# Pacing the transposing DMAs of a planned attention and feed-forward kernel

## The chip, the core and the metric

One NeuronCore of one Trainium2 chip runs the whole kernel. Time is device time in microseconds (us) of one execution; a kernel's time is the median of several executions. Kernel before: 416.09 us, median of 3 runs (414.84 to 416.85).

## What is computed

Eight batches of grouped attention (16 query heads, 4 key/value heads, 384 positions, head size 64), whose output goes through a feed-forward layer with a squared ReLU (1024 to 2048 to 1024). All in float32 outside; the tolerance lets the kernel work in 16 bits.

```python
def _attn_ref(q, k, v):                      # q (8,16,384,64), k and v (8,4,384,64)
    k = np.repeat(k, 4, axis=1); v = np.repeat(v, 4, axis=1)
    scores = np.matmul(q, k.transpose(0, 1, 3, 2)) / np.sqrt(64)
    scores = scores - np.max(scores, axis=-1, keepdims=True)
    attn = np.exp(scores)
    attn = attn / (np.sum(attn, axis=-1, keepdims=True) + 1e-09)
    return np.matmul(attn, v)

def _moe_ref(x, w_in, w_out):                # x (3072,1024)
    h = np.maximum(x @ w_in, 0.0)
    return h * h @ w_out
```

## The kernel before

**A planner writes the order.** The kernel is not written as a sequence of instructions. A class `Recorder` (L9) collects operations with what they read and write, and keeps a planned clock for each engine. `R.add` (L45) gives an operation a start and an end in that plan from a cost in us that the code states; `R.when` (L36) says when given data will be there by the plan. Main loops ask which piece of TensorE work can start now by the plan and record it. In the end `emit` (L86) writes one instruction stream per engine in the order of recording, with semaphore waits where data or buffers require them. So a cost or a due time in the code decides the order that the hardware then runs with its own durations.

**The engines' parts.** TensorE (PE) does all matmuls. ScalarE (ACT) does the exponentials (L402), part of the evictions from PSUM, ReLUs and squares. VectorE (DVE) does most evictions, the normalisation of attention, sums, and some squares. GpSimd (POOL) issues the loads of q, k and v (L239, L264, L271), makes some copies, ReLUs and squares. The sync engine (SP) issues the transposing DMAs, here called turns, and the stores of the output (L933); it takes its queue in order.

**One batch of attention.** Its k, q and v are loaded into `k_st`, `q_st`, `v_st`. Then `prepare(b)` (L1027) puts chores on a list: `dup_k` (L295) copies k twice side by side, `turn_k_dma` (L308) turns it into `kT` with one transposing DMA, two `turn_q_dma` (L315) turn the halves of q into `qT`, and `aug_v` (L304) copies v. When the list is empty, `turned` is set to this batch, and its scores may be recorded. The scores are 18 pieces per batch (`burst_small`, L385), each followed by one exponential on ScalarE into `expT`. `av_halves` (L446) multiplies by v in 8 pieces, VectorE normalises, and `turn_o_dma` (L477) turns the result into `xT` with four more DMAs on SP.

**One batch of the feed-forward layer.** For batches 2 to 7 (SB is 2) the up projection is one level of Strassen's scheme (`strassen`, L744): 28 units, each evicted by `evict` (L765). Four products of each column group end in a ReLU and a square; `close_squares` (L675) decides by the planned clocks where they run. Its plans are named by two letters, the engine of the ReLU and that of the square: "ss" is ScalarE for both, "sg" ScalarE and GpSimd, "gg" GpSimd for both, and "sv", which exists only where no ReLU is left, puts the square on VectorE. The plan with the earliest end is taken. The down projection (`down_halves`, L841) follows and reads the squares `h2T`; its pieces run through `zipped` (L712), whose matmuls have line L802 in the up part and L852 in the down part. Attention of the batches ahead is put between these pieces: scores of batch b may be recorded when the feed-forward layer is at batch b-2 or later, its products with v at batch b-1 or later.

**Upkeep.** Before each step the main loops call `upkeep` (L1108) with the planned clock of TensorE. It records loads of the next batch: for batches 4 to 7 as six pieces (`load_pieces`: k, four of q, v), each waiting for the TensorE operation recorded last (`pe_last`) and at least `LOAD_GAP` = 2.0 us of planned time after the one before. Then, while the first chore's data is expected within 0.5 us, it records chores, several in one call where it can. So the k turn and both q turns of a batch are recorded back to back, and each starts when its data and buffers allow. Scores of a batch are candidates in the last main loop (L1308) from the time at which `R.when` expects their turned data.

Of the kernel before, what the change touches and what calls it, by code (L numbers as in the profile page):

```python
# [141 lines left out]
def bass_gqa_attention__then__ffn_squared_relu_kernel(  # L142
# [24 lines left out]
    SB = 2  # L167
    TINY, DOWN = 2.0 ** -100, 2.0 ** -12

    def at(b):  # L170
        return 1 if b == 1 else 0

    R = Recorder(nc)
# [6 lines left out]
    k_dup = sb("k_dup", [128, NU, 2, D])  # L180
# [6 lines left out]
    hr = [sb(f"hr{i}", [128, S], f32) for i in range(NHR)]  # L187
# [16 lines left out]
    q_st = [sb("q_st", [128, H, NJ * D]).ap(), lead(0, 3072, (H, NJ * D))]  # L204
    qT = [sb("qT", [128, 2 * NU, 128]).ap(), lead(3072, 6144, (2 * NU, 128))]
# [99 lines left out]
        R.add(eng, lambda e: e.tensor_copy(v_aug[b % 2][:, :, 0:D], v_st[at(b)][:, :, :]),  # L305
              reads=[("v_st", at(b))], writes=[("v_aug", b % 2)], cost=0.4 if eng == "vector" else 0.85)

    def turn_k_dma(b):  # L308
        R.add("sync", lambda e: e.dma_start_transpose(
            out=kT[at(b)], in_=k_dup.ap().rearrange("p n x d -> p (n x d)")),  # L310
            reads=[("k_dup", 0, g, x) for g in range(HKV) for x in range(2)],
            writes=[("kT", at(b), g) for g in range(HKV)],
            dma="turn_k", cost=1.4, shared=(8.5, 3.5))

    def turn_q_dma(b, half, after=()):  # L315
        R.add("sync", lambda e: e.dma_start_transpose(
            out=qT[at(b)][:, 12 * half:12 * half + 12, :],
            in_=q_st[at(b)][:, 8 * half:8 * half + 8, :].rearrange("p h e -> p (h e)")),
            reads=[("q_st", at(b), 2 * half + i, x) for i in range(2) for x in range(2)] + list(after),
            writes=[("qT", at(b), 2 * half + i, t) for i in range(2) for t in range(6)], dma=f"turn_q{half}", cost=2.5, shared=(10.0, 4.0))  # L320

    def turn_k_pe(b, g, banks):
        i = pick(banks)
# [53 lines left out]
    def score_reads(b, u, c0=0, n=HC):  # L377
        g = u // NJ
        return [("kT", at(b), g)] + [("kT", at(b), g // 2 * 2, x, y) for x in range(2) for y in range(2) if b == 1] + [("qT", at(b), g, t) for t in range(c0 // 128, (c0 + n) // 128)]
# [295 lines left out]
    def close_squares(which):  # L675

        for x in [x for x in open_squares if which(x)]:
            open_squares.remove(x)
            i, r, dst, keys, relu = x
            val = hr[r].ap()  # L680
            two = val.rearrange("p (f t) -> p f t", f=2)
            end = R.ops[i]["end"]
            act, dve, pool = [max(R.clock[e], end) for e in ("scalar", "vector", "gpsimd")]
            plans = [(act + 0.45 * (1 + relu), "ss"), (max(act + 0.52 * relu, pool) + 0.77 + 0.2, "sg")]
            if relu:
                plans.append((pool + 2.2 + 0.6, "gg"))
            else:
                plans.append((dve + 0.49 + 0.4 + 0.6 * bool(ff["now"]), "sv"))
            one, other = min(plans)[1]
            if relu and one == "s":  # L690
                R.add("scalar", lambda e, val=val: e.activation(val, val, AF.Relu, scale=DOWN * DOWN),  # L691
                      reads=[("hr", r)], writes=[("hr", r)], cost=0.45)
            elif relu:
                R.add("gpsimd", lambda e, val=val: e.tensor_scalar(val, val, DOWN * DOWN, 0.0, ALU.mult, ALU.max),
                      reads=[("hr", r)], writes=[("hr", r)], cost=1.42)
            if other == "s":
                R.add("scalar", lambda e, dst=dst, two=two: e.activation(dst, two, AF.Square),  # L697
                      reads=[("hr", r)], writes=keys, cost=0.45)
            else:
                eng = dict(g="gpsimd", v="vector")[other]  # L700
                n = R.add(eng, lambda e, dst=dst, two=two: e.tensor_tensor(dst, two, two, ALU.mult),
                          reads=[("hr", r)], writes=keys, cost=0.77 if other == "g" else 0.49)
                if other == "v":
                    hr_read[r] = (n,)

# [272 lines left out]
    def warm_up(n, cost):  # L978
        def body(pe):
# [8 lines left out]
          reads=[("k_f32", 0)], writes=[("k_dup", 0, 0, 0)], cost=0.27)  # L988
# [38 lines left out]
    def prepare(b):  # L1027

        chores.append(([("k_st", at(b))], lambda: dup_k(b)))
        chores.append(([("k_dup", 0, 0, 0)], lambda: turn_k_dma(b)))  # L1030
        for half in range(2):
            chores.append(([("q_st", at(b), 2 * half, 0)], lambda half=half: turn_q_dma(b, half)))
        chores.append(([("v_st", at(b))], lambda: aug_v(b, "gpsimd")))
        top_q.append(([("v_st", at(b))], lambda: (top_of(v_st[at(b)].rearrange("p n d -> p (n d)"), ("v_st", at(b))),
                                                  spread_q.append((b, lambda: v_unit(b))))))
# [24 lines left out]
    def open_bank(banks):  # L1060
        return min(R.when(writes=[("bank", i)]) for i in banks)
# [41 lines left out]
    margin = 0.5  # L1103
    since, AMONG = 9, 2
    AV_IN, SC_LATE, SC_IN = 4, 2, 8
    load_pieces, load_at, pe_last, LOAD_GAP = [], [0.0], [], 2.0

    def upkeep(now):  # L1108
        nonlocal loaded, queued, turned
        pe_last[0:1] = [len(R.ops) - 1 - next(i for i, o in enumerate(reversed(R.ops)) if o["eng"] == "tensor")]  # L1110
        if loaded + 1 < B and turned >= loaded and not turn_q and not load_pieces:
            loaded += 1
            if loaded == 2:
                load_k(2)
                load_w_out(1, 0)
                load_w_out(1, 1)
                load_q(2, 0, 8)
                load_q(2, 8, 16)
                load_v(2)
                return False  # L1120
            after = [("qT", (loaded - 1) % 2, HKV - 1, 1)] if loaded > 2 else []
            n = loaded
            if n <= SB + 1:
                load_k(n, after)
                load_q(n, 0, 8)
                load_q(n, 8, 16)
                load_v(n)
            else:
                load_pieces.append(([("k_st", 0)], lambda g: load_k(n, after, g)))
                load_pieces.extend(([("q_st", 0, h // 4, x) for x in range(2)], lambda g, h=h: load_q(n, h, h + 4, after=g))  # L1130
                                   for h in range(0, H, 4))
                load_pieces.append(([("v_st", 0)], lambda g: load_v(n, g)))
        if load_pieces and now >= load_at[0] and R.when(writes=load_pieces[0][0], eng="none") <= now:
            load_pieces.pop(0)[1](tuple(pe_last[0:1]))
            load_at[0] = now + LOAD_GAP
        if not chores and not load_pieces and queued < loaded and (queued - (queued == 1), NU - 1, 5) in scored and pairs >= queued * 8 + 8 * (queued == 1):
            queued += 1
            prepare(queued)
        stretch[0] = split and ff["b"] < SB or bool(ff["now"])
        while chores and R.when(reads=chores[0][0], eng="none") <= now + margin:  # L1140
            chores.pop(0)[1]()
            if not chores:
                turned = queued
        if top_q and (ff["b"] < SB or not ff["now"]) and R.when(reads=top_q[0][0], eng="none") <= now + margin:
            top_q.pop(0)[1]()
        while turned > 1 and held_back:
            held_back.pop(0)()
        close_squares(lambda x: not ff["now"] or R.ops[x[0]]["end"] <= now + 0.2)
        if w_q and w_q[0][0]() and R.when(reads=w_q[0][1], eng="none") <= now and R.clock["vector"] <= now + 0.1:
            w_q.pop(0)[2]()  # L1150
        b = next_sum()
        if b and R.when(reads=[("xT", b % NXT, c) for c in range(NKC)], eng="none") <= now + 0.3:
            summed.add(b)
            sums(b)
        return True
# [152 lines left out]
    while ff["now"] or ff["tiles"] or ff["down"]:  # L1308
# [26 lines left out]
        if sc_q:  # L1335
            b, u = sc_q[0]
            pieces = later[u]
            tiles = {(b, x, t) for x, c0, n in pieces for t in range(c0 // 128, (c0 + n) // 128)}
            bases = [i for i in (0, 2) if not held & {i, i + 1}]
            if turned >= b and b <= ff["b"] + 2 and pairs // 2 * NJ + NEX > b * NU + max(x for _, x, _ in tiles) and bases:  # L1340
                base = min(bases, key=lambda i: max(open_bank([i + x]) for x in range(2)))
                t = max(R.when(reads=[r for p in pieces for r in score_reads(b, *p)]), max(open_bank([base + i]) for i in range(2)))
                cand.append((t, 3, "sc", since_sc >= ((SC_LATE if b == ff["b"] + 1 else SC_IN) if inside else 1)))
        if not cand:
            b = next_sum()
# [66 lines left out]
```

## Time and profile before

| | us |
|---|---|
| median of 3 runs | 416.09 (414.84 to 416.85) |
| the profiled execution, whole | 415.26 |
| its span, first to last instruction | 413.5 |
| last transposed output of batch 7's attention issued | 351.42 |

The profile is of one execution. In its lists a line such as L392 is a line of the kernel: L392 scores, L402 exponentials, L459 products with v, L802 and L852 the two halves of the feed-forward layer, L781 and L786 evictions, L691 and L694 ReLUs, L697 and L701 squares. PEld is TensorE's weight load. A wait is told as who waited for whom; "issue" stands where the profile shows no releaser. "DVE hr L781" means that VectorE's instruction of line 781, which writes the tile `hr`, ended the wait. q, k and v are turned at these times in batches 4 to 7: the k turn of each is issued at 159.84, 198.91, 229.94 and 272.07 us.

### The profile page before, as it was taken

What the parts mean: (1) busy time and instruction counts of PE and PEld (TensorE: products, weight loads), DVE (VectorE), ACT (ScalarE), POOL (GpSimd) and SP (SyncE); (2) the same over time, 40 slices, a digit from 0 to 9 for tenths busy, and PEclk for the clock granted to TensorE, in tenths of its full rate; (3) what the DMA queues carried; (4) which work ended last, traced back from release to release, by engine and by line L of the source; (5) the groups of instructions that cost most, each with busy time, mean ns of one, the idle gap of its engine ahead of it and who ended that gap; (6) DMA issues with size and microseconds to landing.
All of it is one profiled execution on the core that took longest, in us unless ns stands there. A gap on an engine that the chain in (4) does not pass through costs nothing.

```text
span 413.5 us, 14959 instructions
## 1 busy us (share of the span) xinstructions
PE 402.5 (97%) x6880; PEld 298.5 (72%) x6880; DVE 268.7 (65%) x519; ACT 225.6 (55%) x316; POOL 79.3 (19%) x92
## 2 busy tenths in 40 slices
PE   8999999998999999999899999999999999999997
PEld 5566754554648985498755898779987899779844
DVE  3699988999977865368732676427861487337613
ACT  6949610196005883777789378935797066006600
POOL 7680000351210450304030063000220000000000
PEclk9999999999999999999999999999999999999999
DMA  9999999992991119972984795263211221220012
GB/s 176 185 192 188 205 187 177 242 149 42 177 193 54 22 22 111 182 153 22 131 114 103 157 152 65 70 127 113 36 28 52 105 41 24 70 76 31 4 51 103
DMA packets 97072, 44.76 MB, mean 108 GB/s; under 512 B 77424, under 2 KB 90992, under 8 KB 97008
## 3 DMA queue, kind: packets, MB, share of 16 engines
q0 software_dynamic: 36672, 17.44, 33.5%
q1 hardware_dynamic: 59664, 25.86, 29.5%
q8 instruction: 54, 0.88, 0.9%
q10 hardware_dynamic: 672, 0.49, 0.4%
q14 instruction: 10, 0.08, 0.1%
HBM read 35.65 MB, written 12.58 MB: 117 GB/s over the span
## 4 chain that ended last, share of the span: by engine, by line
PE 73%; DMA 14%; DVE 6%; POOL 3%; ACT 2%; issue 1%; SPq 0%; POOLq 0%; DVEq 0%
PE ps L852 27%; PE ps L802 24%; DMA w_out_sb<-in_moe_w_out_dram 9%; PE ps L909 9%; PE ps L392 5%; PE ps L459 5%; DMA wx<-in_v_dram 2%; PE ps L554 2%; DVE h2T L578 1%; DMA qT<-q_st 1%; DMA v_st<-in_v_dram 1%; DVE hr L567 1%; PE ps L418 1%; DVE wx L657 1%; ACT h2T L697 1%
## 5 line engine op out<-in xcount | busy, mean ns | idle before, releaser
L402 ACT ACTIVATE expT<-ps 128x1024 bf16<-128x1024 f32 (+1 forms) x145 | 142.2, 1024 | 60.4 <-PE ps L392 57.7
L852 PE MATMUL ps<-w_out_sb,h2T 64*128 64x512 bf16 x1088 | 136.8, 376 | 0.3 <-ACT h2T L697 0.3
L852 PEld LDWEIGHTS ps<-w_out_sb,h2T 64*128 64x128 bf16 x1088 | 73.5, 94 | 37.5 <-ACT h2T L697 0.8
L802 PE MATMUL ps<-xT,w_in_sb 64*128 64x192 f16 x1152 | 82.6, 243 | 0.6 <-issue 0.5
L930 DVE TENSOR_SCALAR y_sb<-ps,unit 128x512 f32<-128x512 f32 (+2 forms) x37 | 29.4, 796 | 68.8 <-PE ps L852 62.2
L802 PEld LDWEIGHTS ps<-xT,w_in_sb 64*128 64x128 f16 x1152 | 71.0, 94 | 2.2 <-issue 0.8
L392 PE MATMUL ps<-qT,kT 64*128 64x256 bf16 (+2 forms) x336 | 51.9, 324 | 3.6 <-issue 1.7
L802 PE MATMUL ps<-s_sum,wx 64*128 64x192 f16 x768 | 50.9, 243 | 1.0 <-DVE hr L781 0.9
L909 PE MATMUL ps<-w_out_sb,h2T 128*128 128x512 bf16 (+2 forms) x240 | 49.7, 365 | 0.6 <-DVE hr L567 0.5
L786 DVE TENSOR_TENSOR hr<-ps,hr 128x384 f32<-128x384 f32 x72 | 39.5, 555 | 12.7 <-PE ps L802 9.5
L802 PEld LDWEIGHTS ps<-s_sum,wx 64*128 64x128 f16 x768 | 43.8, 94 | 2.3 <-DVE hr L781 1.9
L554 PE MATMUL ps<-xT,w_in_sb 64*128 64x384 bf16 x448 | 42.2, 323 | 0.8 <-DVE hr L567 0.8
L778 ACT COPY hr<-ps 128x384 f32<-128x384 f32 x21 | 10.0, 478 | 57.4 <-PE ps L802 57.4
L909 PEld LDWEIGHTS ps<-w_out_sb,h2T 128*128 128x128 bf16 x240 | 22.3, 98 | 25.8 <-DVE hr L567 0.8
L697 ACT ACTIVATE h2T<-hr 128x384 bf16<-128x384 f32 x74 | 37.8, 521 | 2.5 <-DVE hr L773 0.6
L781 DVE COPY hr<-ps 128x384 f32<-128x384 f32 x51 | 27.9, 556 | 17.0 <-PE ps L802 15.6
L459 PE MATMUL ps<-v_aug,expT 64*128 64x65 bf16 x1440 | 37.8, 190 | 0.0
L691 ACT ACTIVATE hr<-hr 128x384 f32<-128x384 f32 x63 | 32.2, 511 | 9.4 <-DVE hr L786 9.4
L459 PEld LDWEIGHTS ps<-v_aug,expT 64*128 64x128 bf16 x1440 | 34.7, 94 | 2.3 <-DVE o_sb L474 0.2
L554 PEld LDWEIGHTS ps<-xT,w_in_sb 64*128 64x128 bf16 x448 | 22.1, 94 | 15.8 <-DVE hr L567 1.9
L802 PE MATMUL ps<-s_sum,w_in_sb 64*128 64x192 f16 x384 | 32.5, 243 | 0.0
L802 PE MATMUL ps<-xT,wx 64*128 64x192 f16 x384 | 31.7, 243 | 0.0
(86 smaller groups left out, 421.3 us busy)
## 6 DMA issues: line engine op xcount, KB each, us to landing
out_dram<-y_sb SPq DMA_DIRECT2D x47, 256.0 KB, 2.9
w_in_sb<-in_moe_w_in_dram POOLq DMA_DIRECT2D x8, 512.0 KB, 14.9
w_out_sb<-in_moe_w_out_dram POOLq DMA_DIRECT2D x4, 1024.0 KB, 29.5
q_st<-in_q_dram POOLq DMA_DIRECT2D x19, 192.0 KB, 5.0
q_st<-in_q_dram POOLq DMA_DIRECT2D x4, 384.0 KB, 24.7
v_st<-in_v_dram POOLq DMA_DIRECT2D x7, 192.0 KB, 5.5
k_st<-in_k_dram POOLq DMA_DIRECT2D x6, 192.0 KB, 4.7
wx<-in_q_dram POOLq DMA_DIRECT2D x2, 384.0 KB, 7.3
```

The source lines that it names most:

```text
L392: mm = pe.matmul(ps[:, base + x, m * wide:(m + 1) * wide], kT[at(b)][64 * x:64 * x + 64, u, :], q_cols(b, u // NJ, x, c0, c0 + wide))
L402: R.add("scalar", lambda e: e.activation(dst, src, AF.Exp, scale=0.125), reads=keys, writes=[("expT", (b * NU + u) % NEX, t) for u, _, _ i ...
L459: m = pe.matmul(ps[:, p[x], n * DP:n * DP + D + 1], w, v_aug[b % 2][r, g * NJ + j, 0:D + 1], start=(n + j + y == 0), stop=(n + j + y == 2 ...
L554: m = pe.matmul(bank(4 + xs[x])[:, 0:S], w_in_sb[r, kc, c * 128:(c + 1) * 128], xT[b % NXT][r, kc, :], start=(phase < 2 and kc == 0), stop ...
L691: R.add("scalar", lambda e, val=val: e.activation(val, val, AF.Relu, scale=DOWN * DOWN), reads=[("hr", r)], writes=[("hr", r)], cost=0.45)
L697: R.add("scalar", lambda e, dst=dst, two=two: e.activation(dst, two, AF.Square), reads=[("hr", r)], writes=keys, cost=0.45)
L781: R.add("vector", lambda e: e.tensor_copy(hr[r][:, :], src), reads=[("bank", at)], writes=[("hr", r)], cost=0.48, after=hr_read.pop(r, ()))
L786: R.add("vector", lambda e: e.tensor_tensor(hr[r][:, :], src, hr[r][:, :], ALU.add), reads=[("bank", at), ("hr", r)], writes=[("hr", r)], ...
L802: return lambda pe: pe.matmul(bank(at)[:, f * h:f * h + h], w[r, kc, c:c + 128], m[r, kc, :], start=(prod in (1, 5, 2) and y + f + kc == 0 ...
L852: return lambda pe: pe.matmul(bank(at)[:, 0:512], h2T[r, c, i3 * 128:(i3 + 1) * 128], w_out_sb[r, c, x * 512:(x + 1) * 512], start=(y + c ...
L909: m = pe.matmul(bank(i)[:, 0:n], h2T[:, c, i3 * 128:(i3 + 1) * 128], w_out_sb[:, c, c0:c1], start=(c == 0), stop=(c == NFC - 1))
L930: R.add("vector", lambda e: e.tensor_scalar(ysl, bank(i)[:, 0:n], g, g, ALU.mult, ALU.mult), reads=[("bank", i), ("unit", b % 2)], writes= ...
```

## The change

Four edits, all in the planner's rules; the arithmetic is the same.

- Batches 4 to 7 (`b > SB + 1`): the k turn and the q turns carry a wait for the TensorE operation recorded last, and after each the shared time `dma_at` is set to 3.5 us (`TURN_GAP`) past TensorE's planned clock. A paced chore is not recorded before that time.
- Load pieces and paced turns share that time: `load_at` is replaced by `dma_at`, so loads also keep 3.5 us from a turn, and turns 2.0 us from a load.
- Scores of batches 4 to 7 in the last main loop are candidates 3.0 us later than the plan expects their data.
- A square on VectorE is priced at 0.95 us instead of 0.49, both in the choice and in the recorded cost.

```diff
-    def turn_k_dma(b):
+    def turn_k_dma(b, gate=()):
         R.add("sync", lambda e: e.dma_start_transpose(
...
-            dma="turn_k", cost=1.4, shared=(8.5, 3.5))
+            dma="turn_k", cost=1.4, shared=(8.5, 3.5), after=gate)
...
-    def turn_q_dma(b, half, after=()):
+    def turn_q_dma(b, half, after=(), gate=()):
...
-            writes=[...], dma=f"turn_q{half}", cost=2.5, shared=(10.0, 4.0))
+            writes=[...], dma=f"turn_q{half}", cost=2.5, shared=(10.0, 4.0), after=gate)
...
-                plans.append((dve + 0.49 + 0.4 + 0.6 * bool(ff["now"]), "sv"))
+                plans.append((dve + 0.95 + 0.4 + 0.6 * bool(ff["now"]), "sv"))
...
-                          reads=[("hr", r)], writes=keys, cost=0.77 if other == "g" else 0.49)
+                          reads=[("hr", r)], writes=keys, cost=0.77 if other == "g" else 0.95)
...
-        chores.append(([("k_dup", 0, 0, 0)], lambda: turn_k_dma(b)))
+        paced = b > SB + 1
+
+        def go(turn, *args):
+            turn(b, *args, gate=tuple(pe_last) if paced else ())
+            if paced:
+                dma_at[0] = R.clock["tensor"] + TURN_GAP
+
+        chores.append(([("k_dup", 0, 0, 0)], lambda: go(turn_k_dma), paced))
         for half in range(2):
-            chores.append(([("q_st", at(b), 2 * half, 0)], lambda half=half: turn_q_dma(b, half)))
+            chores.append(([("q_st", at(b), 2 * half, 0)], lambda half=half: go(turn_q_dma, half), paced))
...
-    load_pieces, load_at, pe_last, LOAD_GAP = [], [0.0], [], 2.0
+    load_pieces, dma_at, pe_last, LOAD_GAP, TURN_GAP = [], [0.0], [], 2.0, 3.5
...
-        if load_pieces and now >= load_at[0] and R.when(writes=load_pieces[0][0], eng="none") <= now:
+        if load_pieces and now >= dma_at[0] and R.when(writes=load_pieces[0][0], eng="none") <= now:
             load_pieces.pop(0)[1](tuple(pe_last[0:1]))
-            load_at[0] = now + LOAD_GAP
+            dma_at[0] = now + LOAD_GAP
...
-        while chores and R.when(reads=chores[0][0], eng="none") <= now + margin:
+        while chores and R.when(reads=chores[0][0], eng="none") <= now + margin and not (len(chores[0]) > 2 and chores[0][2] and now < dma_at[0]):
...
-                t = max(R.when(reads=[r for p in pieces for r in score_reads(b, *p)]), max(open_bank([base + i]) for i in range(2)))
+                t = max(R.when(reads=[r for p in pieces for r in score_reads(b, *p)]) + 3.0 * (b > SB + 1), max(open_bank([base + i]) for i in range(2)))
```

More of the change, by code (lines that the diff above doesn't have):

```diff
@@ L319, in turn_q_dma @@
             reads=[("q_st", at(b), 2 * half + i, x) for i in range(2) for x in range(2)] + list(after),
-            writes=[("qT", at(b), 2 * half + i, t) for i in range(2) for t in range(6)], dma=f"turn_q{half}", cost=2.5, shared=(10.0, 4.0))
+            writes=[("qT", at(b), 2 * half + i, t) for i in range(2) for t in range(6)], dma=f"turn_q{half}", cost=2.5, shared=(10.0, 4.0), after=gate)
     def turn_k_pe(b, g, banks):
```

## The prediction

> **What bounds the kernel now.** I read the page's busy times first, then the table by stage, then TensorE's waits from 126 us on, where every batch that the change touches is computed.
>
> ```profile
> span 413.5 us, 14959 instructions
> PE 402.5 (97%) x6880; PEld 298.5 (72%) x6880; DVE 268.7 (65%) x519; ACT 225.6 (55%) x316; POOL 79.3 (19%) x92
> ...
> 126.00:155.00 29.00, 28.91 (x719) 26.71 (x720) 21.75 (x43) 23.55 (x34) 10.35 (x9) 1.00 0.13 34
> 155.00:177.00 22.00, 22.00 (x314) 11.44 (x312) 9.78 (x20) 11.82 (x12) 4.48 (x6) 1.00 0.99 155
> 177.00:203.00 26.00, 25.09 (x744) 24.21 (x740) 20.54 (x42) 20.47 (x34) 5.70 (x6) 1.00 0.53 77
> 203.00:229.00 26.00, 24.28 (x258) 13.78 (x256) 9.24 (x19) 21.56 (x24) 4.54 (x6) 1.00 0.73 126
> 229.00:254.00 25.00, 23.46 (x702) 22.61 (x699) 18.41 (x41) 15.36 (x28) 7.23 (x8) 1.00 1.03 143
> ```
>
> Columns of the stages: length, then busy time of PE, PEld, DVE, ACT, POOL, granted clock, DMA share, GB/s. I chose the cuts so that an up projection (the Strassen products, 126:155, 177:203, 229:254) and a down projection (between them) alternate. TensorE is the bound: it is busy for the whole of 155:177 and within 2 us of the whole elsewhere, at clock 1.00. The change adds and removes no matmul, so it can only fill or open holes on TensorE. The holes:
>
> ```profile
> PE ps L392 <- issue: 1.7, 1, 1.7
> PE ps L392 <- DMA qT<-q_st: 1.0, 1, 1.0
> PE ps L802 <- DVE hr L781: 0.9, 1, 0.9
> PE ps L802 <- issue: 0.5, 1, 0.5
> PE ps L852 <- ACT h2T L697: 0.3, 1, 0.3
> ```
>
> These five (total, times, longest) are all that the view of TensorE's waits has after 126 us: 1.7 + 1.0 + 0.9 + 0.5 + 0.3 = 4.4 us, 1.1% of the span. That is the ceiling of any gain.
>
> **The turns and the scores: the first two holes.** For batch 5:
>
> ```profile
> 198.91 2.11 SPq L309 DMA_TRANSPOSE kT<-k_dup  x1
> 201.12 4.77 SPq L316 DMA_TRANSPOSE qT<-q_st  x2
> 205.94 1.48 SPq L479 DMA_TRANSPOSE xT<-o_sb  x1
> ...
> kT<-k_dup SPq DMA_TRANSPOSE x1, 5.5
> qT<-q_st SPq DMA_TRANSPOSE x1, 6.1
> ...
> 204.59 1.02 PE L852 MATMUL ps<-w_out_sb,h2T 64*128 64x512 bf16 x7
> 207.34 0.39 PE L392 MATMUL ps<-qT,kT 64*128 64x512 bf16 x2 [1.72 <-issue]
> 208.41 0.40 PE L392 MATMUL ps<-qT,kT 64*128 64x512 bf16 x2
> ```
>
> SP issues the k turn at 198.91 and the first q turn at 201.12; from issue to landing they take 5.5 and 6.1 us, so q lands at 207.2 and the first score matmul starts at 207.34. The view calls this hole "issue", but its end is the landing. Batch 6:
>
> ```profile
> 229.94 2.03 SPq L309 DMA_TRANSPOSE kT<-k_dup  x1
> 232.07 3.48 SPq L316 DMA_TRANSPOSE qT<-q_st  x2
> ...
> 232.07 5.50 DMA qT<-q_st
> ...
> 237.61 0.39 PE L392 MATMUL ps<-qT,kT 64*128 64x512 bf16 x2 [1.01 <-DMA qT<-q_st]
> ```
>
> Here the q turn lands at 232.07 + 5.50 = 237.57. Call T the issue of the k turn: q's first half is there at T+8.3 (batch 5) and T+7.6 (batch 6). The planner's costs in the code, with no load in flight, expect it at 0.1 + 0.8 + 1.4 + 2.5 + 1.5 = T+6.3. So the plan is 2.0 and 1.3 us too early, and the holes are 1.72 and 1.01: the same cause twice.
>
> With the change, the q half is recorded 3.5 us after the k turn, behind a wait for TensorE's latest work. The plan then expects it at 3.5 + 0.1 + 0.8 + 2.5 + 1.5 = T+8.4, and the added 3.0 puts the first score at T+11.4. By the row of 6.1 it lands at T+9.6, so 1.8 us are spare. If another SP issue stands ahead of it (1.48, the xT turn above), 0.3 is left; with the second half's share of 4.77 there as well nothing is, and about 1 us of the wait would come back. I take the full gain, **-1.72 and -1.01**, since each turn now stands alone, and keep 0 for the range.
>
> What the waits hold up: behind a gated turn in SP's queue stand stores and the xT turns of the batch before. The turn at 205.94 is batch 4's last, and its reader starts here:
>
> ```profile
> 228.80 0.24 PE L802 MATMUL ps<-xT,w_in_sb 64*128 64x192 f16 x1
> ```
>
> That is 22.9 us after issue, so a delay by the spread of 7 us costs nothing; uncovered, the whole 7 us would stand on TensorE.
>
> **What is late next.** Scores start at T+11.4 instead of T+6.3, 5.1 us later. TensorE has other matmuls to run, so the delay moves work and adds none. Where the exponentials go:
>
> ```profile
> L402 ACT ACTIVATE expT<-ps x10: 1005/1023/1031, 176.8 to 197.0; 128x1024 bf16<-128x1024 f32 x10
> ...
> 126.00:155.00 29.00, 15.75 (x16) 1.00 0.13 34
> 155.00:177.00 22.00, 10.46 (x11) 1.00 0.99 155
> 177.00:203.00 26.00, 9.98 (x10) 1.00 0.53 77
> 203.00:229.00 26.00, 18.41 (x18) 1.00 0.73 126
> 229.00:254.00 25.00, 4.67 (x5) 1.00 1.03 143
> ```
>
> In a down stage a score comes every 1.07 us (207.34 to 208.41), in an up stage every 2.2 us (ten from 176.8 to 197.0). Five of batch 4's scores slip from 155:177 to 177:203, which then has 15. The stage 126:155 already carries 16 exponentials and ACT 23.55 of 29.00 us, with PE 28.91 busy, so I cost this at **0**. The cover is ACT's free 26.0 - 20.47 = 5.5 us against 5 x 1.02 = 5.1.
>
> **Loads.** Batch 6's loads and the turn after them:
>
> ```profile
> 207.90 0.74 POOL L271 DMA_DIRECT2D q_st<-in_q_dram  x1 [9.48 <-PE ps L392]
> ...
> 216.45 0.74 POOL L264 DMA_DIRECT2D v_st<-in_v_dram  x1 [1.40 <-PE ps L392]
> ```
>
> Pieces already came about 2 us apart and the last was issued 13.5 us before the turn at 229.94. Now the six start at T+10.5 and end at T+20.5. The next T may then come from T+26 by the loads, or from T+11.4 + 18 x 1.07 = T+30.7 by the scores; the measured step is 229.94 - 198.91 = 31.0. Batch 6 may slip by several us, inside the 22.9 of slack: **0**.
>
> **Squares.** The third hole:
>
> ```profile
> L701 DVE TENSOR_TENSOR h2T<-hr x13: 548/550/1195, 139.5 to 390.7; 128x384 bf16<-128x384 f32 x13
> L701 POOL TENSOR_TENSOR h2T<-hr x9: 826/827/1232, 137.8 to 304.1; 128x384 bf16<-128x384 f32 x9
> ...
> 189.47 1.46 POOL L300 COPY k_dup<-k_st 128x1536 bf16<-128x1536 bf16 x1
> 190.88 1.15 POOL L305 COPY v_aug<-v_st 128x768 bf16<-128x768 bf16 x1
> 190.36 2.08 DVE L701 TENSOR_TENSOR h2T<-hr 128x384 bf16<-128x384 f32 x2
> 193.16 1.08 PE L802 MATMUL ps<-s_sum,wx 64*128 64x192 f16 x22 [0.91 <-DVE hr L781]
> ...
> L697 ACT ACTIVATE h2T<-hr 128x384 bf16<-128x384 f32 x74 | 37.8, 521 | 2.5 <-DVE hr L773 0.6
> ```
>
> Two squares take VectorE 2.08 us beside GpSimd's copies instead of 2 x 0.55, the eviction L781 behind them is late, and TensorE waits 0.91. At a planned price of 0.95 the planner gives nearly all thirteen to ACT (0.52 each) or GpSimd (0.83), and the eviction is free: **-0.91**. Nothing excludes that another queue holds up an eviction instead, so the low end is 0. Price of the move: in the last batch TensorE already waits for ACT's square (0.3); two more there cost 0 to 1.04. I take **+0.3**, one such wait again.
>
> The Trainium skill, page "SBUF — State Buffer", section "Who interferes with whom", says that a VectorE instruction with two SBUF inputs contends with a GpSimd one that reads SBUF, and that the later one blocks; the rows agree (1.195 against 0.548). By it squares moved to GpSimd would still meet VectorE's remaining two-input work, and -0.91 would shrink; that is the third rival below.
>
> **Sum.** -1.72 - 1.01 - 0.91 + 0.3 = -3.34 on the profiled execution of 415.26 us (its span is 413.5; 1.76 lie around it) gives 411.92. That execution is 0.83 below the median of the runs, 416.09, so I forecast 416.09 - 3.34 = **412.8**. Its own range: 411.5 (every hole, -4.4, would be 411.7) to 414.3, when half is given back.
>
> **Rivals.**
>
> *ScalarE becomes the bound in 177:203 (slower).* Place: evictions and squares behind exponentials. For it: the stage has only 5.5 us of ACT left, and 5 exponentials with two squares take 5.1 + 1.04 = 6.1. It decides as soon as more than five scores slip. If all eleven do, ACT needs 20.47 + 11 x 1.02 + 1.04 = 32.7 in 26.0, so 6.7 us are lost: 416.09 - 2.73 + 6.7 = 420.1. Against it: 126:155 lived with 16.
>
> *The waits move (no change).* Q is still late: a q turn gated by TensorE and stuck behind SP's other issues lands at T+11.4 or after, and scores pressed into fewer slots open holes elsewhere. For it: two turns' issue takes 4.77 us of SP. Gain left 0.6: 415.5.
>
> *Squares end on GpSimd.* Its squares and VectorE's two-input work block each other as now, -0.91 vanishes, and the +0.3 stays: 416.09 - 2.73 + 0.3 = 413.7. Against it: GpSimd's own squares mostly ran at 0.827, undisturbed.
>
> *The edit hardly acts* (turns were already late behind other waits, so pacing orders nothing new): 416.1. Against it: turn issues follow each other within 2.2 us now and must then stand 3.5 apart.
>
> **From these to the numbers.** Forecast 0.45, squares on GpSimd 0.10, waits move 0.20, no effect 0.05, ScalarE 0.20. I call 0.5% (2.08 us) what a measurement can tell: faster below 414.0, slower above 418.2. Nearly all of the first, most of the second and a little of the third lie below 414.0: 0.58. ScalarE's case reaches from about 417 to 420: 0.18 slower. Same: 0.24. The range is 411.0 to 418.5: below by the ceiling of 4.4 and the spread of runs, above into the ScalarE case without its upper half.
>
> **What would show it.** Right: SP's k and q turns stand about 3.5 us apart in batches 4 to 7, no wait of L392 for qT, hardly any L701 on DVE, and TensorE's waits after 126 us total about 1 to 1.5 us. Wrong: a hole of PE L802 or L852 behind ACT L697, L691 or POOL L701, or ACT over 25 us in the third batch's up stage; or a new late resource ahead of the scores.

## The result and the profile after

| | before | after |
|---|---|---|
| median of 6 runs, us | 416.02 (414.84 to 416.85) | 410.79 (409.2 to 411.07) |
| the profiled execution, us | 415.26 | 410.94 |
| its span, us | 413.5 | 409.1 |

The ratio is 0.9867, with a 95% interval of 0.9844 to 0.989: the change makes the kernel faster by 5.2 us (4.6 to 6.5). A second set of runs gave 411.44 against 416.78, ratio 0.987 (0.9831 to 0.991). Some runs had a mean granted clock of 0.992 or 0.996 instead of 1.000 and were mostly longer: 8 of the 54 runs of the kernel before that stand beside the experiments (417.31 to 420.17 us), five of the twelve runs of the experiment P alone below (416.07 to 417.61, where the other seven have a median of 414.33), and none of the 12 of the changed kernel. The forecast was 412.8: the side is right, the size too small, and the time lies 0.21 below the range's low end of 411.0.

From the page of the changed kernel, span and busy times:

```profile
span 409.1 us, 14961 instructions
...
PE 401.6 (98%) x6880; PEld 286.3 (70%) x6880; DVE 271.3 (66%) x526; ACT 213.5 (52%) x296; POOL 91.9 (22%) x105
```

The same 6880 matmuls took 402.5 us of "busy" before and 401.6 now. So 0.9 of the 4.4 us that the span lost were booked as work, not as waits. This is the first sign that the waits told less than the whole.

TensorE's waits after 126 us, changed kernel (total, times, longest):

```profile
PE ps L802 <- issue: 0.9, 1, 0.9
PE ps L852 <- ACT h2T L697: 0.3, 1, 0.3
```

Both waits for qT and the one behind L781 are gone; ACT L697's wait in the last batch is as before. The hole of 0.9 is new, or rather moved (before had 0.5 of that kind); the last section is on it.

The sync engine's work for batch 5, and the first scores of that batch, changed kernel:

```profile
206.47 1.74 SPq L309 DMA_TRANSPOSE kT<-k_dup  x1
210.02 0.34 SPq L933 DMA_DIRECT2D out_dram<-y_sb  x1
210.72 1.22 SPq L479 DMA_TRANSPOSE xT<-o_sb  x1
211.99 0.57 SPq L933 DMA_DIRECT2D out_dram<-y_sb  x1
212.66 3.65 SPq L316 DMA_TRANSPOSE qT<-q_st  x2
...
DMA to landing us min/median/max: 5.0/5.4/5.8
...
216.16 4.48 PE L852 MATMUL ps<-w_out_sb,h2T 64*128 64x512 bf16 x40
220.47 0.38 PE L392 MATMUL ps<-qT,kT 64*128 64x512 bf16 x2
```

With T the issue of the k turn (206.47), the first q turn goes out at T+6.2, behind a store and an xT turn, and lands by 212.66 + 5.8 = 218.5, which is T+12.0. The first score runs at T+14.0 with no wait. The two q turns still leave as a pair, 2.0 us apart.

The same stretches of work before and after: each window reaches from the first Strassen product of one batch (3, 4) to that of the next. Before:

```profile
176.01:228.80 52.79, 50.16 (x1020) 38.75 (x1014) 30.33 (x61) 42.35 (x57) 10.91 (x12) 1.00 0.64 106
228.80:278.33 49.53, 47.99 (x989) 41.77 (x983) 28.17 (x60) 31.78 (x45) 10.56 (x11) 1.00 0.68 109
```

After:

```profile
174.06:221.77 47.71, 47.71 (x981) 35.84 (x978) 28.87 (x60) 28.98 (x42) 12.21 (x13) 1.00 0.65 100
221.77:270.56 48.79, 47.89 (x981) 35.77 (x978) 28.87 (x60) 29.02 (x42) 12.23 (x13) 1.00 0.53 96
```

ACT's column (the fourth pair) fell from 42.35 of 52.79 to 28.98 of 47.71, and TensorE is busy for the whole of the first window. Attention now runs at the same pace as the feed-forward layer: the k turns stand at 158.82, 206.47, 255.26 and 302.98 (48 to 49 apart), where before they were 39, 31 and 42 apart.

**A list of holes from start to start.** In the profile the ends of TensorE's matmuls are modelled, so a wait that is counted from the record's end is too short. The fence above shows it: forty L852 matmuls take 4.48 us. Their single records start in pairs, so one pair follows another after (4.48 - 0.38) / 19 = 0.216 us, though each record is 0.38 long. Before, the last pair ahead of batch 5's hole started at 205.18 and the next could have started at 205.40, so the hole up to 207.34 was 1.94 long and not 1.72. I therefore took, from the start times of all matmuls after 126 us, how much later each started than the rate of its form allows:

```text
                                          before   after
scores wait for q, batch 5 (207.34)        1.94      -
scores wait for q, batch 6 (237.61)        1.18      -
behind squares: 193.16                     1.09      -
                153.64                     0.31      -
                381.95                     0.30      -
                293.70 and 294.86          0.35      -
no releaser ("issue", L802)                0.73     1.07
in both: L802, ACT L697, L909              0.97     0.97
all delays under 0.12 us together          5.71     6.15
sum                                       12.58     8.19
```

The difference is 4.39, and the stretch from the first Strassen product to the end is 4.38 shorter (287.17 against 282.79). The four lines behind squares add 2.05, of which TensorE's waits showed only the first. The waits of the weight loads, whose records are only 0.09 us long, do show more of them. Before, then after:

```profile
PEld ps L802 <- DVE hr L781: 1.9, 3, 1.1
...
PEld ps L852 <- POOL h2T L701: 0.6, 1, 0.6
```

```profile
PEld ps L802 <- issue: 1.1, 1, 1.1
PEld ps L852 <- ACT h2T L697: 0.8, 1, 0.8
```

Three waits behind L781 and one behind GpSimd's square stood there, and none stands there now. How a square makes the hole at 293.70, on VectorE before:

```profile
291.81 1.18 DVE L701 TENSOR_TENSOR h2T<-hr 128x384 bf16<-128x384 f32 x1
293.09 1.02 DVE L781 COPY hr<-ps 128x384 f32<-128x384 f32 x2
```

The square takes 1.18 instead of 0.55, beside one of GpSimd's own squares (291.75, 0.83 long), and the evictions behind it are late. The square ahead of the hole at 381.95 is not slow: it takes 0.55 and only stands ahead of the eviction that TensorE waits for. The hole at 153.64 is of another kind: TensorE itself waits for a square on GpSimd.

### The profile page after: what moved, and what is told of

It is laid out like the page before. It is cut to its first block, busy times and chain, and to the rows that moved or that the text cites. A ratio compares the mean times of both kernels' runs of the same rounds, so it can differ in the third digit from the quotient of the medians.

```text
span 409.1 us, 14961 instructions
## 1 busy us (share of the span) xinstructions
PE 401.6 (98%) x6880; PEld 286.3 (70%) x6880; DVE 271.3 (66%) x526; ACT 213.5 (52%) x296; POOL 91.9 (22%) x105
## 4 chain that ended last, share of the span: by engine, by line
PE 84%; DMA 6%; DVE 4%; POOL 2%; ACT 1%; issue 0%; ACTq 0%
PE ps L852 28%; PE ps L802 27%; PE ps L909 12%; PE ps L392 6%; PE ps L459 5%; DMA w_in_sb<-in_moe_w_in_dram 5%; PE ps L554 5%; PE ps L418 2%; DVE h2T L578 1%; DVE hr L567 1%; DMA wx<-in_k_dram 1%; POOL w_in_sb L282 1%; DVE wx L657 1%; ACT h2T L697 1%; DVE wx L652 1%; ACT hr L691 1%
## 5 line engine op out<-in xcount | busy, mean ns | idle before, releaser
L402 ACT ACTIVATE expT<-ps 128x1024 bf16<-128x1024 f32 (+1 forms) x145 | 140.6, 1026 | 108.2 <-PE ps L392 107.1
L852 PE MATMUL ps<-w_out_sb,h2T 64*128 64x512 bf16 x1088 | 133.8, 376 | 0.3 <-ACT h2T L697 0.3
L852 PEld LDWEIGHTS ps<-w_out_sb,h2T 64*128 64x128 bf16 x1088 | 60.4, 94 | 47.0 <-ACT h2T L697 0.8
L802 PE MATMUL ps<-xT,w_in_sb 64*128 64x192 f16 x1152 | 86.6, 243 | 1.0 <-issue 0.9
L930 DVE TENSOR_SCALAR y_sb<-ps,unit 128x512 f32<-128x512 f32 (+2 forms) x37 | 29.4, 795 | 45.0 <-PE ps L852 38.1
L802 PE MATMUL ps<-s_sum,wx 64*128 64x192 f16 x768 | 52.5, 243 | 0.0
L694 POOL TENSOR_SCALAR hr<-hr 128x384 f32<-128x384 f32 x16 | 23.9, 1491 | 97.8 <-DVE hr L786 97.8
L781 DVE COPY hr<-ps 128x384 f32<-128x384 f32 x60 | 33.0, 557 | 16.1 <-PE ps L802 14.4
L697 ACT ACTIVATE h2T<-hr 128x384 bf16<-128x384 f32 x69 | 35.3, 521 | 1.8
L802 PE MATMUL ps<-s_sum,w_in_sb 64*128 64x192 f16 x384 | 34.4, 243 | 0.0
L691 ACT ACTIVATE hr<-hr 128x384 f32<-128x384 f32 x56 | 28.7, 513 | 2.9 <-DVE hr L786 2.9
```

What stands on the lines that cost most here:

```text
L402: R.add("scalar", lambda e: e.activation(dst, src, AF.Exp, scale=0.125), reads=keys, writes=[("expT", (b * NU + u) % NEX, t) for u, _, _ i ...
L781: R.add("vector", lambda e: e.tensor_copy(hr[r][:, :], src), reads=[("bank", at)], writes=[("hr", r)], cost=0.48, after=hr_read.pop(r, ()))
L802: return lambda pe: pe.matmul(bank(at)[:, f * h:f * h + h], w[r, kc, c:c + 128], m[r, kc, :], start=(prod in (1, 5, 2) and y + f + kc == 0 ...
L852: return lambda pe: pe.matmul(bank(at)[:, 0:512], h2T[r, c, i3 * 128:(i3 + 1) * 128], w_out_sb[r, c, x * 512:(x + 1) * 512], start=(y + c ...
L930: R.add("vector", lambda e: e.tensor_scalar(ysl, bank(i)[:, 0:n], g, g, ALU.mult, ALU.mult), reads=[("bank", i), ("unit", b % 2)], writes= ...
```

## The experiments

Three edits can be made one at a time: S, the scores' 3.0 us; P, the paced turns with their gate and the shared `dma_at`; Q, the price of 0.95 for a square. The ratios are against the kernel before, run beside each.

**S alone**

```diff
-                t = max(R.when(reads=[... score_reads(b, *p)]), ...)
+                t = max(R.when(reads=[... score_reads(b, *p)]) + 3.0 * (b > SB + 1), ...)
```

> Only the 3.0 us that hold scores back; turns back to back, loads and squares as before. Hole theory (the gain is the sum of the holes on TensorE that an edit closes): q lands 1.3 to 2.0 us later than planned in batches 5 and 6, 3.0 covers both, so 1.72 + 1.01 are gone and the hole of 0.9 behind the two squares stays: 416.0 - 2.7 = 413.3. Rival, step theory (the gain comes from pacing and delay together, which bring one batch of attention per batch of the feed-forward layer): under 1 us of gain, 415 to 416.

414.36 us (413.61 to 415.79), ratio 0.9947 (0.9924 to 0.997); this lies between the two expectations. TensorE's waits after 126 us:

```profile
PE ps L617 <- DVE top_w L607: 2.0, 1, 2.0
PE ps L852 <- ACT h2T L697: 0.8, 2, 0.5
...
PE ps L802 <- DVE hr L781: 0.6, 2, 0.4
```

The q waits are gone, as the delay alone should do. But a new hole of 2.0 us stands at 256.14: L617, a small matmul that spreads the largest value of a batch's v, waits for VectorE, and VectorE for the load of v:

```profile
249.58 0.74 POOL L264 DMA_DIRECT2D v_st<-in_v_dram  x1 [1.51 <-PE ps L459]
...
256.78 0.95 DVE L605 TENSOR_REDUCE top<-v_st 128x1 f32<-128x768 bf16 x1 [3.52 <-DMA v_st<-in_v_dram]
```

The load is the last of its six, held back by its wait for TensorE, and takes 7.2 us to land. A second new hole, 0.72 us at 204.10, is of the kind that the rival with ScalarE named: L852 waits for a square on ACT that stands behind two exponentials. In this profile S gains less than in the runs: without the holes that have no releaser, the stretch from the first Strassen product to the end is 285.7 us long, against 286.44 before. What makes the rest of the 2.2 us between the medians (414.36 and 416.62) is not shown.

**P alone**

```diff
 (against the changed kernel, lines abbreviated)
-... + 3.0 * (b > SB + 1) ...
-... dve + 0.95 ... cost=0.77 if other == "g" else 0.95 ...
+... dve + 0.49 ... cost=0.77 if other == "g" else 0.49 ...
```

> Only paced turns with the shared time for loads; scores are candidates when the plan expects q, squares at 0.49. Hole theory: the plan expects q's first half 4.9 us after its own issue, the chip needs 4.0 to 6.1, so at most a hole of about 1 us is left of 2.73: 416.0 - 1.7 to - 2.7 = 413.3 to 414.3. Step theory: under 1 us of gain, 415 to 416.

415.61 us (413.49 to 417.61), ratio 0.9958 (0.9928 to 0.9988). Waits, and SP's queue for batch 7:

```profile
PE ps L392 <- DMA qT<-q_st: 1.5, 1, 1.5
...
276.48 1.46 SPq L309 DMA_TRANSPOSE kT<-k_dup  x1
278.00 0.56 SPq L933 DMA_DIRECT2D out_dram<-y_sb  x1
278.68 2.59 SPq L316 DMA_TRANSPOSE qT<-q_st  x1
281.31 1.29 SPq L479 DMA_TRANSPOSE xT<-o_sb  x1
282.71 2.63 SPq L316 DMA_TRANSPOSE qT<-q_st  x1
```

Pacing alone leaves one q wait, in batch 7: the turn of 278.68 lands when the first score starts, at 285.2, 6.5 us after issue, with its k turn 2.2 us ahead and the next issue 2.6 us behind it. So a paced turn can be as slow as one in a burst (6.1 before). The plan expects the first half of q 4.9 us after its issue; in P's batches 4 to 7 it took 3.95, 3.80, 5.43 and 6.51. Where that is too short, the 3.0 us on the scores are what covers it. The median is the one that the step theory gave, but the ratio is worth 1.8 us, and in the profile the stretch to the end is 2 us shorter (284.3 against 286.44), as the hole theory has it.

**Q alone, and the change without Q**

```diff
-                plans.append((dve + 0.49 + 0.4 + 0.6 * bool(ff["now"]), "sv"))
+                plans.append((dve + 0.95 + 0.4 + 0.6 * bool(ff["now"]), "sv"))
...
-                          ..., cost=0.77 if other == "g" else 0.49)
+                          ..., cost=0.77 if other == "g" else 0.95)
```

> Only the price of 0.95 for a square on VectorE. Hole theory: the hole of 0.91 behind the two slow squares goes, the two behind q stay: 415.1. Rival (the price does nothing, since 11 of 13 squares stay on VectorE in the changed kernel): 416.0 within 0.4, with a hole of the same kind in another place.

414.43 us (412.28 to 418.01), ratio 0.9946 (0.9915 to 0.9977), so 2.2 us (1.0 to 3.5): more than the 0.9 of the hole theory, and the rival's nothing is excluded. The q waits stay (the first row), the long wait behind L781 and the one behind POOL L701 are gone; weight loads' waits of this kernel:

```profile
PEld ps L392 <- DMA qT<-q_st: 3.7, 3, 2.2
...
PEld ps L802 <- DVE hr L781: 0.7, 2, 0.4
```

This profile is of the longest of the twelve executions (418.01 us). Right behind a wait for q of 2.1 us, which ends at 203.87, the granted clock is 0.5 for 3.4 us (the column behind POOL's pair):

```profile
204.40:207.80 3.40, 3.40 (x40) 2.07 (x37) 2.42 (x6) 1.33 (x2) 0.76 (x2) 0.50 0.84 120
```

In it pairs of L852 start every 0.43 us instead of 0.216, so about 1.7 us of work are lost (an estimate: half of 3.4). One such stretch makes the mean of this execution 0.996. None of the other profiles has one, and why the clock fell is not shown.

> The changed kernel with a square on VectorE back at 0.49. Hole theory, if the price is worth its 0.9: 410.8 + 0.9 = 411.7. Rival (pacing moves the copies on GpSimd away from the squares, so the price is worth nothing): 410.8 within 0.5, and no square on VectorE over 0.7 us.

413.53 us (411.17 to 414.56), ratio 0.9915 (0.9884 to 0.9947). Squares and weight loads' waits of this kernel:

```profile
L701 DVE TENSOR_TENSOR h2T<-hr x16: 546/548/1217, 140.1 to 388.6; 128x384 bf16<-128x384 f32 x16
...
PEld ps L392 <- DVE o_sb L474: 1.1, 2, 0.8
...
PEld ps L802 <- DVE hr L781: 0.8, 3, 0.4
...
PEld ps L852 <- POOL h2T L701: 0.6, 1, 0.6
```

The holes behind squares are back with the old price: 0.31 at 154.27, 0.48 at 204.43, 0.13 at 241.24 and 0.30 at 379.81, 1.2 in all from start to start. By the ratios (0.9915 against 0.9867) Q is worth 0.5% on top of the other two, 2.0 us, though these two intervals overlap a little. Together with Q alone (at least 1.0) this makes it likely that the price of the squares is worth more than the 0.6 of the forecast; where it lies between the 1.2 of these holes and 2.2 is not settled.

**The change again, without its gate, and the kernel before again**

```diff
-            turn(b, *args, gate=tuple(pe_last) if paced else ())
+            turn(b, *args, gate=())
```

> The changed kernel once more, beside the kernel before on the same chip as the next three. Measurement theory (part of the 5.2 is that the first profiled execution of the kernel before was 0.8 quicker than its median, while the changed kernel scatters less): changed kernel 410.8 within 0.5 and its runs within 2.5 us of each other, those of the kernel before over 3 us apart. Rival: the changed kernel scatters as much, and the first six runs were lucky: median 411.5 to 413.

411.44 us (410.35 to 412.51), ratio 0.987 (0.9831 to 0.991). The median lies between the two expectations; the runs are 2.2 us apart, those of the kernel before 5.2.

> The changed kernel without the wait for TensorE on the turns; order of recording unchanged. Order theory (the gain lies in the order of work that the rules give, and the wait itself does nothing): 410.8 within 0.5. Rival (the wait keeps turns from colliding with loads on the chip): turns are issued up to 3 us earlier in the trace, land later than 6 us after issue, and the time rises by 1 us or more.

411.39 us (410.98 to 411.9), ratio 0.987 (0.9833 to 0.9907). The order of the instructions is the same with and without the gate, and so is the time (411.44 beside it). Batch 5's turns on SP without the gate:

```profile
206.86 1.95 SPq L309 DMA_TRANSPOSE kT<-k_dup  x1
210.46 0.34 SPq L933 DMA_DIRECT2D out_dram<-y_sb  x1
211.15 1.22 SPq L479 DMA_TRANSPOSE xT<-o_sb  x1
212.41 0.57 SPq L933 DMA_DIRECT2D out_dram<-y_sb  x1
213.08 3.55 SPq L316 DMA_TRANSPOSE qT<-q_st  x2
```

The q turns go out at T+6.2 here too. So what pacing does, it does by the order in which turns and loads are recorded; the waits that the turns carry do nothing that the time shows.

> The kernel before, for a second profile. Measurement theory: holes behind q in batches 5 and 6 again (1 to 3 us together), and a hole that no semaphore ends in another place or of another size; the span is up to 3 us from 413.5, and the steps from batch to batch show in which. Rival: the same holes at the same places within 0.2 us, and a difference of the span, if any, lies ahead of 126 us.

One run, 415.89 us. Every hole with a releaser returned at its place, with its size to within 0.25 us (for instance 1.09 at 192.47, 1.71 at 206.41, 1.19 at 236.69, 0.31 at 153.07), but not those without one. Waits of this execution:

```profile
PE ps L459 <- issue: 1.5, 1, 1.5
...
PE ps L802 <- issue: 0.3, 1, 0.3
```

From start to start these are 1.69 and 0.53, against one of 0.73 in the first profile: 1.5 us of difference between two executions of one program. Without these holes, the stretch from the first Strassen product to the end is 286.44 and 286.15 before, and 281.72 and 281.75 after (two profiles each).

**The loads**

```diff
-    load_pieces, dma_at, pe_last, LOAD_GAP, TURN_GAP = [], [0.0], [], 2.0, 3.5
+    load_pieces, dma_at, pe_last, LOAD_GAP, TURN_GAP = [], [0.0], [], 4.0, 3.5
```

> The changed kernel with 4.0 us instead of 2.0 between load pieces; nothing else. Fetch theory (the hole of 0.90 on TensorE at 230 us, which no semaphore ends, is TensorE waiting for its own instructions, whose 16 KB packet came late behind load packets): with the DMA engines half idle the hole goes, the step of batch 4 falls from 48.8 to 47.7 us, 410.8 - 1.0 = 409.8. Rival (the hole is something else, such as a full queue of TensorE): the hole stays and the time is 410.8 within 0.4.

410.97 us (409.41 to 411.27), ratio 0.9848 (0.9806 to 0.989). The hole without a releaser is 0.56 now and at another place (190.35).

> The changed kernel with 3.0 us between load pieces. Fetch theory: a part of the holes without a semaphore goes, 410 to 411, between the changed kernel and the one with 4.0. Rival: no order among 2.0, 3.0 and 4.0.

With 3.0: 410.72 us (410.54 to 411.04), ratio 0.9865 (0.9838 to 0.9892); three such holes of 0.30 to 0.38. Neither is told apart from the change itself. With one profile each, it is not shown that spreading the loads makes these holes smaller or fewer, and no version found beats the changed kernel by more than the runs can tell.

```diff
-        st = at(b)
+        st, n = at(b), 1 if b > SB + 2 else HKV
...
-            k_st[st].rearrange("p (g j) d -> p g (j d)", j=NJ),
-            k[b].rearrange("g (p j) d -> p g (j d)", j=NJ)),
+            k_st[st][:, 0:n * NJ, :].rearrange("p (g j) d -> p g (j d)", j=NJ),
+            k[b, 0:n].rearrange("g (p j) d -> p g (j d)", j=NJ)),
```

The same is done to the loads of q and v.

> The changed kernel, but the loads of k, q and v of batches 5 to 7 move only one head of four (the rest of the tiles keeps older data, so the output of these batches is another); every instruction and wait stays in its place. Fetch theory: with a quarter of the load packets TensorE's own 16 KB packets are no longer late, no hole without a semaphore is left after 170 us, every step from batch 3 to 6 is 47.7 us, and the time falls by the 1.1 to 1.6 us of such holes, to 409.5 to 410.2. Rival (those holes have nothing to do with DMA traffic): they stay, at other places or the same, and the time is 410.8 to 411.4.

410.67 us (410.03 to 411.13), ratio 0.9856 (0.9828 to 0.9884). TensorE's only wait after 126 us, and the window that matches 221.77:270.56 above:

```profile
PE ps L852 <- ACT h2T L697: 0.3, 1, 0.3
...
223.03:270.75 47.72, 47.72 (x982) 35.87 (x979) 28.85 (x60) 28.92 (x42) 10.94 (x13) 1.00 0.37 82
```

No hole without a releaser is left, and the batch takes 47.72 instead of 48.79: the 1.07 are gone with three quarters of the load packets. The time does not show it: 410.67 lies above the expected 409.5 to 410.2 and is not told apart from the change. The evidence is this one profile, without such a hole where the thirteen others have one to four.

**Two of three: without pacing, without the delay**

```diff
 (without pacing: the kernel before with the lines of S and Q above)
 (without the delay: against the changed kernel, line abbreviated)
-... + 3.0 * (b > SB + 1) ...
```

> Scores 3.0 us later and the square at 0.95, but turns back to back and loads on their own time, as before. Sum theory (each edit closes the holes that have its cause, and the three add up): without pacing the two holes behind q are still closed by the delay, so at most 1 us over the changed kernel: 411 to 412. Rival, step theory (pacing and delay together bring attention into one batch per batch of the feed-forward layer): as the scores alone did, a new hole of about 2 us behind a late load of v, and 413 to 414.5.

411.27 us (410.08 to 413.97), ratio 0.9883 (0.9854 to 0.9912); waits:

```profile
PE ps L802 <- issue: 1.0, 1, 1.0
PE ps L852 <- DVE y_sb L930: 0.9, 1, 0.9
```

The time is the sum theory's. The new hole is another than the late v of S alone: TensorE waits for VectorE's L930.

> Paced turns and the square at 0.95, but scores as early as the plan expects q. Sum theory: a hole of 1.2 to 1.7 us behind a q turn stays in one batch, the rest is closed: 412 to 413. Rival, step theory: attention runs ahead of the feed-forward layer again, the last turn of k comes at about 277 instead of 303 us, several holes stay, and 413 to 415.

411.17 us (410.69 to 411.87), ratio 0.9875 (0.9851 to 0.9899); waits:

```profile
PE ps L392 <- DMA qT<-q_st: 1.3, 1, 1.3
```

The one hole behind a q turn came as the sum theory has it, though the time is below its 412 to 413. The last column is the stretch from the first Strassen product to the end in the profiled execution, without the holes that have no releaser; for Q alone the stretch at half clock makes it useless.

| edits made | ratio | interval | stretch, us |
|---|---|---|---|
| none | 1 | | 286.44, 286.15 |
| S | 0.9947 | 0.9924 to 0.997 | 285.7 |
| P | 0.9958 | 0.9928 to 0.9988 | 284.3 |
| Q | 0.9946 | 0.9915 to 0.9977 | - |
| S, P | 0.9915 | 0.9884 to 0.9947 | 282.6 |
| S, Q | 0.9883 | 0.9854 to 0.9912 | 282.3 |
| P, Q | 0.9875 | 0.9851 to 0.9899 | 282.9 |
| S, P, Q | 0.9867 | 0.9844 to 0.989 | 281.72, 281.75 |

Each edit alone is worth about 0.5%, and two of them about 1%. The third seems to add less (0.1% over P and Q, 0.16% over S and Q), but the intervals are too wide to say so. The profiles are sharper: two profiles of the whole change agree within 0.03 us and two of the kernel before within 0.3, and each pair of edits takes 0.6 (S, Q), 0.9 (S, P) or 1.2 us (P, Q) longer, so in the traces each edit still closes something on top of the other two. The even step of 47.7 us per batch is not what makes the gain: S with Q takes 48.9, 50.7 and 49.4 us for batches 2 to 4, the whole change 47.7, 47.7 and 48.8, and their ratios are 0.16% apart.

## Why the prediction was right in kind and wrong in size

**The bound, and where the gain comes from: right.** The change only closed holes on TensorE. Those the prediction named closed: S alone removes the q waits, P alone leaves one in another batch (1.5 us, batch 7), and without Q the slow squares come back. TensorE's listed waits fell to 0.9 + 0.3 = 1.2 us, as forecast, but the 0.9 is a hole of another kind than those it named.

**The step that failed: "1.7 + 1.0 + 0.9 + 0.5 + 0.3 = 4.4 us ... That is the ceiling of any gain".** It took the waits of a pipelined engine for all of its lost time. They are counted from modelled ends, which hides about 0.2 us of each hole and all of the smaller ones. The Trainium skill, page "Perfetto Trace Analysis", section "Tensor Engine Instruction (MATMUL, LD_WEIGHTS)", says that the end of a matmul in the profile is estimated, not observed. No run here shows the true end; the trace shows that the told durations overlap (0.38 us told, one pair every 0.216 us). Term by term:

| term | forecast | measured from start to start |
|---|---|---|
| q wait of batch 5 | -1.72 | -1.94 |
| q wait of batch 6 | -1.01 | -1.18 |
| squares | -0.91 | -2.05 |
| given back in the last batch | +0.3 | 0 |
| holes without a releaser | 0 | +0.34 (0.73 to 1.07) |
| delays under 0.12 us | 0 | +0.44 |
| sum | -3.34 | -4.39 |

The term for the squares is the one most mis-sized: it held one of four places at which a square stood in the way. Q alone (2.2 us) and the 1.2 us of holes that return without Q go the same way. What the 0.44 consist of stays open. The holes of the named kinds were worth 5.17 where the list had 3.64; that the net of 4.39 equals the "ceiling" of 4.4 is chance, since the ceiling also counted two waits that did not close.

**The step that took the time below the range: "That execution is 0.83 below the median".** With the whole ceiling of 4.4 the forecast would have been 411.7, still inside the range. The sum was carried over to the median as if this distance were a constant. It is 416.02 - 415.26 = 0.76 by the later median, but the changed kernel's profiled execution lies 0.15 above its own median. These 0.91, the 0.98 between -3.34 and the profiled difference of 415.26 - 410.94 = 4.32, and the 0.07 by which the median of before moved make up the whole miss of 412.75 - 410.79 = 1.96. The 0.91 was not traced to one place. Runs at a lower granted clock account for little of it: without them the kernel before's 33 runs beside S, P and Q have a median of 416.44 instead of 416.62. Holes without a releaser scatter by 1.5 us between executions of one program, and the start of the first Strassen product lay between 125.65 and 127.58 us over the profiles.

**The turns: right in the end, wrong in the path.** The prediction had the q half land at T+9.6 and the first score at T+11.4. They came at T+12.0 and T+14.0: in SP's queue two stores and an xT turn stood ahead of the q turns, with or without the gate. This is what the rival "the waits move" feared, but the scores moved as far, so 2.0 us were spare where 1.8 were forecast: two errors, of 2.4 and 2.6 us, cancelled, and that is luck. "SP's k and q turns stand about 3.5 us apart" did not come true: k to q is 6.2 to 7.2 in batches 4 to 7, q to q about 2. "Each turn now stands alone" holds in part: the first q turn of batches 4, 6 and 7 lands after 4.0 us, where it took 5.7, 5.5 and 4.5, but batch 5's still takes 5.8 (6.1 before), with the next turn 2.0 us behind it.

**Squares: effect right, way wrong.** "Nearly all thirteen" were to leave VectorE; eleven are there (changed kernel):

```profile
L701 POOL TENSOR_TENSOR h2T<-hr x16: 825/827/945, 137.8 to 345.0; 128x384 bf16<-128x384 f32 x16
L701 DVE TENSOR_TENSOR h2T<-hr x11: 548/549/558, 139.5 to 385.9; 128x384 bf16<-128x384 f32 x11
```

None of the eleven is slow: the longest takes 558 ns, where it took 1195. None of them starts while GpSimd copies or squares; six start during a ReLU on GpSimd (L694) and keep their 548 to 558 ns. The new price alone does not do this: each kernel with only one or two of the edits still has two to four squares on VectorE of 707 to 1217 ns (in Q alone three of ten). This is also why the rival "squares end on GpSimd" fell: sixteen squares are there, up from nine, and nothing waits for one.

**Right at no cost:** loads, the xT turns and stores in SP's queue, and the five later scores opened no hole in the changed kernel. In S alone a late load of v and a square on ACT did (2.0 and 0.72 us). With the shared sequence of P no profile had that hole, though S with Q and without P had none either, so what keeps v in time was not told apart.

**ScalarE as the bound: wrong.** ACT needs at most 29.02 us in a step of 47 to 49. The rival had the delay press eleven scores into an up stage. What came instead is that attention took a slower, even pace, with k turns 48 to 49 us apart instead of 31 to 42, and ACT's load in the steps of batches 2 to 5 evened out: 28.01 to 29.02 where it was 29.73 to 42.35. In the up stage the rival looked at, ACT's load did rise, to 24.70 of 27.94 us (174.06:202.00), and TensorE was busy for all 27.94.

## What to carry to other kernels

Take TensorE's holes from the starts of its matmuls or from the weight loads, not from the waits behind modelled ends; here the sum over listed waits was no ceiling. Where a planner's prices set the order, look for every place at which the mispriced instruction delays something, small ones too. A forecast for the median should not carry the one profiled execution's distance from it over as a constant.

## What the hardware showed: TensorE waits for its own instructions

The hole of 0.90 in the chain of waits of the changed kernel, with no releaser, and the queues' packets in 227:231.5:

```profile
229.46 0.58 PE ps L802 x14
230.04 0.90 issue
230.94 0.59 PE ps L802 x10
...
q0 software_dynamic: 1406, 0.52, 112.3%
q8 instruction: 1, 0.02, 1.2%
```

The instruction queue moves 54 packets of 16 KB in a whole execution (0.88 MB). TensorE has 13,760 matmuls and weight loads and 52 recorded waits: about 64 bytes for each, so 256 to a packet. The packet of this stretch runs from 228.55 to 229.45, and TensorE goes on at 230.94, 1.5 us behind its end. Over the 14 profiles, 27 holes of 0.2 to 1.8 us after 126 us look alike: each ends 1.3 to 1.7 us behind the end of such a packet, and the number of TensorE instructions, waits included, that ran before it is always 0.73 to 0.76 of 256 past a multiple of 256. Thirteen profiles have one to four of them; the one with a quarter of the load packets has none. The packet ahead of each hole is late: it starts when TensorE is 0.32 to 0.71 of 256 instructions past the last such place; of the other 575 packets after 126 us, 56 start so late. So TensorE most likely runs out of instructions when a packet of its own is late among the packets of the loads, which fill the DMA engines there (queue 0's packets are put at 112.3% of the 16 engines' time in this window). Why it is at 0.73 to 0.76, and what takes the 1.3 to 1.7 us, stays open.

The Trainium skill, page "Runtime: NRT & Kernel Launch", section "Instruction fetch mechanics", says that instructions come in blocks of 16 KiB, 256 of them, and that the cost at a block's end is mostly hidden. The size agrees with the trace, and so does "mostly": of 54 blocks one to four show in one execution. Beside heavy loads the cost is not always hidden, and after 126 us it is what differs most between two profiles of one kernel: 0.73 and 2.2 us for the kernel before, 1.07 and 1.6 for the changed one.
